# Attention and a three-layer chain on one core: TensorE in program order in one stretch

## The chip, the cores and the metric

The kernel runs on one core of a Trainium2 chip. The metric is the device time of one execution in microseconds, as the median of several runs. The engines have a queue each and work side by side: TensorE (PE in the rows; PEld are its weight loads) multiplies matrices and transposes, VectorE (DVE), ScalarE (ACT) and GpSimd (POOL) work on rows, SyncE (SP) issues most DMAs. Semaphores hold an instruction back until its inputs are there or its output buffer is free.

## The reference

Three layers follow each other.

```python
# 1 attention, B=4 batches, 8 heads, 512 local and 32 global tokens, 64 wide
out_g = softmax(q_g @ [k_g; k_l].T / 8) @ [v_g; v_l]
out_l = softmax([q_l @ k_g.T, masked(q_l @ k_l.T)] / 8) @ [v_g; v_l]   # |i-j| <= 32
x = concat(out_g, out_l)                  # 4 * 544 rows of 512
# 2 two products
x = leaky(x @ w_in) @ w_out               # 512 -> 2048 -> 512, leaky(h) = max(0.01 h, h)
# 3 soft mixture, 8 experts with 4 slots each
logits = x @ phi                          # 32 columns
d = softmax over rows (logits)            # dispatch, needs all rows
slots = d.T @ x
y = relu(slots @ w1[e]) @ w2[e]           # per expert
return softmax over columns (logits) @ y
```

## The kernel before

**Work and tiles.** The 2176 rows are 17 tiles of 128: tiles 0 to 15 are four per batch, tile 16 holds the global tokens of all batches. Layer 2's second product is never made for itself. With U = d.T @ leaky(h) and a matrix pmat = w_out @ phi that is made beforehand, the logits come from leaky(h) directly (`lg`), and U is summed over the tiles with a running maximum.

**Attention** goes by steps of a batch and a pair of heads (`step`, 4 per batch). `a_T` transposes k and q (tiles kTp and qTp), `a_S` makes 32 small products (sc, L434), each with 32 queries and a window of 96 keys and 32 global ones. VectorE masks them and takes the maximum (L446), ScalarE makes eight exponentials (L454). `a_E` transposes those (etp, copied out as eT), `a_V` makes 32 small products with v (po, L493). In the third step of a batch `g_S` makes the logits of global attention (gl, gg); after the fourth `g_E` transposes its exponentials (get, geg: L561, L565) and `g_V` multiplies (gpo, L579) and transposes the result (gxt, L592).

**A tile of layers 2 and 3.** `b_X` transposes a tile of x (xtp) and splits it in a coarse and a fine part. `b_H` makes H for a quarter f of 512 columns: 12 products of 128x512 in a bank hp (L691), in two half pieces of six, then ScalarE's Prelu (L698). For two quarters of a tile `blocks` transposes on VectorE and copies on GpSimd; `b_L` transposes the other two on TensorE (gtp). `b_D1` sums the logits (lg, L742) and copies them as lp. `b_D2` multiplies lp once more (L757), takes the running maximum (L761 on VectorE) and makes the exponential st (L766 on ScalarE, part of it copied by L767 on VectorE). `b_D3` transposes st (L802) and cuts out d; `b_U` multiplies d with the tile's g (up, L812) and adds it to U.

**Order.** `b_items` writes a list of items of weight and function for tiles 4 to 14: the half pieces h[0] to h[7] of a tile's H, and between them li[0] to li[5], the logits and U of the tile before: li[1] is `b_L`, li[2] to li[5] are `b_D1`, `b_D2`, `b_D3` and `b_U`; li[0] does nothing for these tiles. `merge` interleaves the steps of attention for batches 2 and 3 with that list by their weights. That is only the order of the program text. A scheduler then sets the order of every engine's queue by its own estimate of times, and puts what is ready in front of what waits; `held` and `behind` keep an item behind a named TensorE instruction. The last branch of `b_items` is for tiles 5 to 10, those beside attention.

**Buffers** on which the order bears: the transposes xtp, kTp, qTp, etp, gtp, get, geg and gg share two PSUM banks (`tp`), H and a few up share two (`hb`), sc and gl two (`sc`), po, gpo and the later up one (`po`).

Of the kernel before, what the change touches and what calls it, by code (L numbers as in the profile page):

```python
# [20 lines left out]
def kernel(  # L21
# [16 lines left out]
    B, H, S, D = q_l.shape  # L38
# [4 lines left out]
    NT = S // P  # L43
# [220 lines left out]
    class Stream:  # L264
# [15 lines left out]
        def next(self, dst=None, half=None):  # L280
            self.start()
            self.ahead = max(self.ahead - 1, RING)
            r = convert(self.pool, self.raw.pop(0), dst, half)
            return r
# [343 lines left out]
    def step(n):  # L628

        b, i = order[n]  # L630
        last = i == NP - 1
        e = (0.9, lambda: a_E(b, i))
        v = (1.6, lambda: (a_V(b, i), None if n < NP else load_vn(b) if i == NP - 2 else load_v(n + (1 if last else 2))))
        ns = [(2.7, lambda: a_S(*order[n + 1]))] if n + 1 < NN else []
        nt = [(0.9, lambda: T_(n + 2))] if n + 2 < NN else []
        if not last:
            gs = [(2.2, lambda: g_S(b))] if i == NP - 2 else []
            return ns + [e] + gs + nt + [v]
        gv = (2.1, lambda: (g_V(b), load_v(n + 2) if b else None))
        return [e, (0, lambda: None), v, (1.1, lambda: g_E(b))] + ns + nt + [gv]  # L640
# [11 lines left out]
    def b_X(t):  # L652
        if seq[t] is None:
            pt = xg0.rearrange("p k t -> p (k t)")
        else:
            b, T = seq[t]
            pt = tp("xtp")
            for i in range(KD):
                nc.tensor.transpose(  # L659
                    pt[:, P * i:P * i + P],  # L660
                    xn[b][:, T, 2 * i:2 * i + 2, :].rearrange("p h d -> p (h d)"), ident,
                )
        pool, tags = (sa, ("qn", "kn")) if t == 2 else (sb, ("xh", "xl"))
        xh, xl = (pool.tile([P, KD, P], F32R, tag=g, name="x" + g, bufs=2) for g in tags)
        nc.scalar.mul(xh.rearrange("p k t -> p (k t)"), pt, WS)  # L665
        nc.vector.scalar_tensor_tensor(
            out=xl.rearrange("p k t -> p (k t)"), in0=pt, scalar=WS,
            in1=xh.rearrange("p k t -> p (k t)"), op0=ALU.mult, op1=ALU.subtract,
        )
        xt[t] = (xh, xl)  # L670
# [3 lines left out]
    def b_H(t, f, half=None):  # L674
        xh, xl = xt[t]
        if half != 1:
            if f == 0:
                gt[t] = (
                    xa.tile([P, FF], F32, tag="xn", name="gx", bufs=1) if t in (3, NTT - 1)
                    else sa.tile([P, FF], F32, tag="vw", name="g2", bufs=2) if t == 2  # L680
                    else sb.tile([P, FF], F32, tag="g", name="g", bufs=2)
                )
            hps[0] = hb("hp")
        hp = hps[0]
        w = wi[f]
        lo, hi = {None: (0, KD), 0: (0, KD // 2), 1: (KD // 2, KD)}[half]
        prods = [(k, a, c) for k in range(lo, hi) for a, c in ((xh, 0), (xh, 1), (xl, 0))]
        if t == NTT - 1:
            prods.sort(key=lambda x: -x[2])
        for n, (k, a, c) in enumerate(prods):  # L690
            nc.tensor.matmul(  # L691
                hp, a[:, k, :], w[c][:, k, :],
                start=(n == 0 and half != 1), stop=(n == len(prods) - 1 and half != 0),
            )
        if half == 0:
            return
        gs = gt[t][:, 512 * f:512 * f + 512]
        nc.scalar.activation(out=gs, in_=hp, func=AF.Prelu, alpha=0.01)  # L698
        if t in BLK or t in HALF and f < 2:
            blocks(t, f, gs)  # L700
# [196 lines left out]
    def l_items(t):  # L897
        return ([(0.0, lambda: None), (0.6, lambda: b_M(t, range(2)))] if t in BLK else [
            (0.0, lambda: None) if t in HALF else (0.9, lambda: (b_L(t, 0), b_L(t, 1))),
            (0.9, lambda: (b_L(t, 2), b_L(t, 3))),  # L900
        ]) + [
            (1.3, lambda: b_D1(t)),
            (0.3, lambda: b_D2(t)),
            (0.1, lambda: b_D3(t)),
            (1.0, lambda: b_U(t)),
        ]
# [49 lines left out]
    def behind(item):  # L956
        def go():
            with tc.issue_after(ms["b"]):
                item[1]()
        return (item[0], go) + item[2:]  # L960

    def held(item):
        def go():
            with tc.issue_after(last_a[0]):
                item[1]()
        return (item[0], go)

    def b_items(t0, t1):
        its = []
        for t in range(t0, t1):  # L970
            li = l_items(t - 1)
            h = [held((1.3, lambda t=t, f=f, a=a: b_H(t, f, a))) for f in range(NQ) for a in range(2)]
            x = [(0.5, lambda t=t: b_X(t + 1), t + 1)] if t + 1 < NTT else []
            if t == NT:
                its += h[0:4] + x + h[4:]
                continue
            if t - 1 in BLK:
                its += h[0:2] + [li[1]] + h[2:4] + [li[2]] + x + [behind(h[4])]
                its += [li[3]] + [behind(x) for x in h[5:8]] + [li[4], li[5]]
                continue  # L980
            its += h[0:2] + [li[0]] + h[2:4] + [li[1]] + h[4:5] + x + h[5:6]
            its += [li[2], h[6], li[3], h[7], li[4], (0.0, lambda: None), li[5]]
        return its

    def merge(a, c):
        ta, tb = sum(x[0] for x in a) or 1.0, sum(x[0] for x in c) or 1.0
        pa = pb = 0.0
        a, c = list(a), list(c)
        while a or c:
            if a and (not c or pa / ta <= pb / tb):  # L990
                w, f = a.pop(0)[:2]
                pa += w
            else:
                w, f = c.pop(0)[:2]
                pb += w
            f()
# [20 lines left out]
    def run(*items):  # L1017
        for x in items:
            x[1]()
# [48 lines left out]
    attn = [None] + [sum((step(n) for n in range(NP * b, NP * b + NP)), []) for b in range(2, B)]  # L1068
    LB = NTT - 2
    rest = b_items(NT, LB)  # L1070

    def upto(t):
        n = next(n for n, x in enumerate(rest) if x[2:] == (t,))
        head = rest[:n]
        del rest[:n]
        return head

    for b in range(2, B):
        head = upto(b * NT if b == 2 else 3 * NT - 1)
        merge(attn[b - 1], head[:-6])  # L1080
        run(*head[-6:])
    actx.close()


# [93 lines left out]
    li = l_items(LB - 1)  # L1178
# [140 lines left out]
    for m, (c0, c1) in enumerate(((0, CL), (CL, 512))):  # L1319
# [24 lines left out]
        for n, ts in enumerate(order2):  # L1344
# [17 lines left out]
            else:  # L1362
                ob = obp.pop(0).rearrange("p (t c) -> p t c", c=W)
                copy(ob, opv)
                b, T = seq[ts[0]]
# [39 lines left out]
```

## Time and profile before

| | |
|---|---|
| median of 3 runs | 492.21 us (492.15 to 493.1) |
| profiled execution | 493.25 us, its span 491.5 us |
| TensorE busy in the span | 457.3 us (93%) |
| VectorE, ScalarE, GpSimd busy | 272.2, 232.8, 159.5 us |
[...]

The loop over batches 2 and 3 is the stretch from 189.0 to 344.4 us after the start of the span. [...] The difference of two starts in the timeline is the time that a group really took; a length beside a start reaches a little into the next group, because products are pipelined.

### The profile page before, as it was taken

How to read it: one execution, taken by the hardware profiler on the slowest of the kernel's cores; microseconds unless marked ns; L12 is line 12 of the kernel's file. 1: busy time of each engine (PE TensorE's matmuls, PEld its weight loads, DVE VectorE, ACT ScalarE, POOL GpSimd, SP SyncE). 2: the span in 40 equal slices, each digit the busy share in tenths (PEclk: the TensorE clock that was granted, in tenths of full speed). 3: DMA queues.
4: the chain of work that ended last, by engine and by line, in shares of the span. 5: the costliest groups of instructions: out<-in, count | busy, mean ns of one | idle time of the engine just before them, and what ended most of it. 6: DMA issues, size and time to landing. Idle time of an engine off the chain costs nothing.

```text
span 491.5 us, 13458 instructions
## 1 busy us (share of the span) xinstructions
PE 457.3 (93%) x5341; PEld 319.0 (65%) x5341; DVE 272.2 (55%) x880; ACT 232.8 (47%) x678; POOL 159.5 (32%) x281
## 2 busy tenths in 40 slices
PE   7967789998989999999999999999999999999982
PEld 5645568676766666776777776877777777743341
DVE  4676868489547676566554646435755542242223
ACT  4766889487754444445155526224533343321021
POOL 2044877333310202632415251515766630000000
PEclk9987889999989999999999999999999999999998
DMA  9989597499654565442450211229720059989997
GB/s 178 228 200 264 191 290 299 155 308 298 209 145 104 117 145 91 101 103 79 110 108 2 59 40 22 87 91 394 289 86 1 2 184 342 391 324 398 349 305 255
DMA packets 111990, 90.23 MB, mean 184 GB/s; under 512 B 75256, under 2 KB 94392, under 8 KB 111928
## 3 DMA queue, kind: packets, MB, share of 16 engines
q1 hardware_dynamic: 110024, 88.33, 61.5%
q10 hardware_dynamic: 1904, 1.05, 0.8%
q8 instruction: 42, 0.69, 0.6%
q14 instruction: 20, 0.16, 0.1%
HBM read 76.68 MB, written 8.65 MB: 174 GB/s over the span
## 4 chain that ended last, share of the span: by engine, by line
PE 77%; DVE 4%; ACT 3%; DMA 3%; issue 1%; SPq 1%; POOL 0%; DVEq 0%; ACTq 0%; POOLq 0%
PE hp L691 39%; PE gtp L728 4%; PE sc L434 3%; PE up L812 3%; PE ehp L1269 3%; PE po L493 3%; PE lg L742 3%; PE etp L473 2%; PE sop L1303 1%; PE gpo L579 1%; DMA wo_f<-wo 1%; PE qTp L390 1%; PE sop L1325 1%; PE lg L916 1%; PE xtp L659 1%; PE gl L519 1%
## 5 line engine op out<-in xcount | busy, mean ns | idle before, releaser
L691 PE MATMUL hp<-wi,xxh 128*128 128x512 f32 x512 | 167.2, 407 | 1.3 <-ACT xxh L665 1.3
L691 PEld LDWEIGHTS hp<-wi,xxh 128*128 128x128 f32 x512 | 91.8, 190 | 28.9 <-issue 9.1
L719 POOL COPY g<-gb 32x256 f32<-32x256 f32 x206 | 82.9, 402 | 82.6 <-DVE gb L710 55.5
L691 PE MATMUL hp<-wi,xxl 128*128 128x512 f32 x256 | 101.2, 396 | 0.0
L698 ACT ACTIVATE g<-hp 128x512 f32<-128x512 f32 x60 | 35.4, 597 | 57.9 <-PE hp L691 56.0
L454 ACT ACTIVATE se<-se,nmx 128x128 f32<-128x128 f32 x128 | 49.6, 391 | 21.2 <-DVE nmx L452 21.1
L691 PEld LDWEIGHTS hp<-wi,xxl 128*128 128x128 f32 x256 | 48.3, 189 | 11.9 <-issue 0.8
L200 POOL COPY vw<-vw 32x1664 f32<-32x1664 f32 x10 | 15.8, 1576 | 79.5 <-DMA vw<-in_v_l_dram 24.6
L446 DVE CUSTOM_DVE_ANT_0 se<-sc,mask 128x128 f32<-128x128 f32 x128 | 28.9, 284 | 12.1 <-PE sc L434 12.0
L261 POOL TENSOR_TENSOR wn<-wn,rraw 128x512 int32<-128x512 int32 x16 | 22.6, 1424 | 34.4 <-DVE wn L257 31.1
L710 DVE STREAM_TRANSPOSE gb<-g 128x512 f32<-128x512 f32 x32 | 22.3, 704 | 19.3 <-ACT g L698 14.0
L434 PE MATMUL sc<-kw,qT 64*32 64x128 f32 x1024 | 29.1, 283 | 0.4 <-DVE mx L446 0.4
L493 PE MATMUL po<-vw,eT 128*32 128x64 f32 x1024 | 23.7, 228 | 3.9 <-issue 3.2
L261 POOL TENSOR_TENSOR wo<-wo,rraw 128x512 int32<-128x512 int32 x12 | 15.7, 1310 | 32.3 <-DVE wo L257 8.9
L434 PEld LDWEIGHTS sc<-kw,qT 64*32 64x32 f32 x1024 | 19.8, 109 | 8.4 <-issue 5.4
L493 PEld LDWEIGHTS po<-vw,eT 128*32 128x32 f32 x1024 | 17.8, 113 | 10.4 <-issue 8.8
L477 DVE COPY eT<-etp 128x512 f32<-128x512 f32 x28 | 18.7, 685 | 10.0 <-PE etp L473 9.9
L454 ACT ACTIVATION_READ_ACCUMULATOR se<-se,nmx 128x1 f32 x128 | 24.2, 189 | 0.0
L473 PE MATMUL etp<-identr,se 128*128 128x128 f32 x128 | 22.7, 297 | 0.3
L405 DVE COPY kw<-kT 128x672 f32<-128x672 f32 x32 | 19.5, 644 | 3.1 <-ACT kT L394 2.9
L251 ACT ACTIVATE rraw<-rraw 128x512 int32<-128x512 uint32 x28 | 18.7, 681 | 4.0 <-POOL wo L261 2.8
L730 ACT COPY gT<-gtp 128x512 f32<-128x512 f32 x26 | 14.8, 586 | 10.8 <-PE gtp L728 7.0
(228 smaller groups left out, 764.7 us busy)
## 6 DMA issues: line engine op xcount, KB each, us to landing
ew<-in_moe_w_dram SPq DMA_DIRECT2D x23, 1024.0 KB, 8.4
rraw<-in_moe_w_in_dram SPq DMA_DIRECT2D x16, 512.0 KB, 6.4
ew<-in_moe_w_dram SPq DMA_DIRECT2D x15, 512.0 KB, 8.8
vw<-in_v_l_dram SPq DMA_DIRECT2D x60, 112.0 KB, 3.5
rraw<-in_moe_w_out_dram SPq DMA_DIRECT2D x12, 512.0 KB, 5.8
wo_f<-wo SPq DMA_DIRECT2D x16, 256.0 KB, 3.7
vn<-in_v_l_dram SPq DMA_DIRECT2D x4, 1024.0 KB, 6.2
wo<-wo_f SPq DMA_DIRECT2D x4, 1024.0 KB, 7.8
```

The source lines that it names most:

```text
L261: nc.gpsimd.tensor_tensor(out=di, in0=di, in1=m, op=ALU.add)
L405: nc.vector.tensor_copy(kw[:, :, 0:96], src)
L434: last_a[0] = nc.tensor.matmul(bks[e][32 * u:32 * u + 32, P * T:P * T + P], qt[64 * e:64 * e + 64, 32 * U:32 * U + 32], kw[win(U) // (NW / ...
L446: nc.vector.tensor_tensor_reduce(out=s[:, T, :], in0=bk[:, P * T:P * T + P], in1=mask[:, 0 if T == 0 else 2 if T == NT - 1 else 1, :], sca ...
L454: exp_last[0] = nc.scalar.activation(out=s[:, T, :], in_=s[:, T, :], func=AF.Exp, bias=nmx[:, e, T:T + 1], accum_out=sm[:, T, e:e + 1],).ins
L473: last_a[0] = nc.tensor.transpose(pt[:, P * T:P * T + P], es[e][:, T, :], ident).ins
L493: last_a[0] = nc.tensor.matmul(pov[32 * u:32 * u + 32, T, e, :], ets[e][:, 32 * U:32 * U + 32], vw[:, win(U), e, :], start=True, stop=True ...
L691: nc.tensor.matmul(hp, a[:, k, :], w[c][:, k, :], start=(n == 0 and half != 1), stop=(n == len(prods) - 1 and half != 0),)
L698: nc.scalar.activation(out=gs, in_=hp, func=AF.Prelu, alpha=0.01)
L710: nc.vector.transpose(out=gb[:, f % 2], in_=gs)
L719: copy(dst[32 * c:32 * c + 32, :, a], src[32 * a:32 * a + 32, :, c])
L728: nc.tensor.transpose(pt[:, P * c:P * c + P], g[:, o:o + P], ident)
```

## The change

Two edits. The items of tiles 5 to 10 are put in another order, and the loop over batches 2 and 3 is traced inside a block in which the scheduler leaves TensorE's queue in program order. The other engines' queues are still set by the scheduler.

```diff
@@ b_items, tiles 5 to 10
-            its += h[0:2] + [li[0]] + h[2:4] + [li[1]] + h[4:5] + x + h[5:6]
-            its += [li[2], h[6], li[3], h[7], li[4], (0.0, lambda: None), li[5]]
+            its += [h[0], li[1], h[1], li[0], h[2], h[3], li[2]] + x + [h[4], li[3]]
+            its += [h[5], h[6], li[4], h[7], li[5]]
@@ the loop over batches 2 and 3
-    for b in range(2, B):
-        head = upto(b * NT if b == 2 else 3 * NT - 1)
-        merge(attn[b - 1], head[:-6])
-        run(*head[-6:])
+    with tc.manual_schedule(engines={mybir.EngineType.PE}):
+        for b in range(2, B):
+            head = upto(b * NT if b == 2 else 3 * NT - 1)
+            merge(attn[b - 1], head[:-6])
+            run(*head[-6:])
```

First place: TensorE's queue where global attention of batch 2 ends. Before, the transposes of global attention's exponentials (get, geg) stand apart, the second pair behind passes of sc and lg:

```order
L434 MATMUL sc_3648<-kw,qT 32x128
L434 MATMUL sc_3647<-kw,qT 32x128
L434 MATMUL sc_3648<-kw,qT 32x128
L742 MATMUL lg<-g_3101,pmat 32x128 x8
L561 MATMUL get<-identr,gs 128x128 x4
L565 MATMUL geg<-identr,gs 32x128
L742 MATMUL lg<-gT,pmat 32x128 x8
L691 MATMUL hp<-wi,xxh 128x512 x2
```

In the changed program the same transposes, and those of the next tile of x, read:

```order
L561 MATMUL get<-identr,gs 128x128 x4
L565 MATMUL geg<-identr,gs 32x128
L561 MATMUL get<-identr,gs 128x128 x4
L565 MATMUL geg<-identr,gs 32x128
L659 MATMUL xtp<-identr,xn 128x128 x4
L691 MATMUL hp<-wi,xxh 128x512 x2
```

The sc and lg that lay between have moved: sc stands undivided behind the half piece of H that follows, lg undivided ahead.

Second place: a little later on TensorE, where st of tile 6 is transposed (L802) and global attention's result too (gxt). Before:

```order
L434 MATMUL sc_3919<-kw,qT 32x128
L434 MATMUL sc_3920<-kw,qT 32x128
L434 MATMUL sc_3919<-kw,qT 32x128
L592 MATMUL gxt<-identr,xg 128x128
L802 MATMUL lg<-identr,st 128x128
L728 MATMUL gtp<-identr,g 128x128 x4
L434 MATMUL sc_3920<-kw,qT 32x128
```

After, from the last products of the sc of the step before (3661 and 3662) up to L802:

```order
L434 MATMUL sc_3661<-kw,qT 32x128
L434 MATMUL sc_3662<-kw,qT 32x128
L757 MATMUL lg<-lp,s_77 128x128
L691 MATMUL hp<-wi,xxh 128x512 x2
L691 MATMUL hp<-wi,xxl 128x512
L691 MATMUL hp<-wi,xxh 128x512 x2
L691 MATMUL hp<-wi,xxl 128x512
...
L390 MATMUL kTp<-identr,kn 128x128 x4
L390 MATMUL qTp<-identr,qn 128x128 x4
L802 MATMUL lg<-identr,st 128x128
```

Four more rows of H (the second half piece) stand where the line of dots is. Behind L802 come a half piece of H, the whole of gpo and then gxt:

```order
L691 MATMUL hp<-wi,xxl 128x512
L579 MATMUL gpo<-vn,get 32x64 x16
L579 MATMUL gpo<-vg,geg 32x64 x4
L579 MATMUL gpo<-vn,get 32x64 x16
L579 MATMUL gpo<-vg,geg 32x64 x4
L592 MATMUL gxt<-identr,xg 128x128
L812 MATMUL up<-g,d 32x512 x4
```

What moved: the passes of the next sc lie no longer between gpo and gxt or around L802, and L802 stands two half pieces of H and two transposes behind L757, where before gpo, qTp, a half piece and passes of sc lay between them.

Third place: ScalarE's queue at the same point. The eight exponentials of attention (se) are those of the sc above. Before:

```order
L454 ACTIVATE se,sm<-se,nmx 128x128 x8
L665 ACTIVATE xxh<-xtp 128x512
L394 ACTIVATE kT<-kTp 128x512
L766 ACTIVATE st,zt<-lg,nm 128x128
L771 ACTIVATE al<-al 128x1
```

After:

```order
L454 ACTIVATE se,sm<-se,nmx 128x128 x8
L766 ACTIVATE st,zt<-lg,nm 128x128
L771 ACTIVATE al<-al 128x1
L394 ACTIVATE kT<-kTp 128x512
L394 ACTIVATE qT<-qTp 128x512
```

st has moved up to the place right behind the eight; kT is behind it now.

## Rows read from the trace of the kernel before

**Rows 1.** The page's chain of waits, shares of the span by engine.

```profile
PE 77%; DVE 4%; ACT 3%; DMA 3%; issue 1%; SPq 1%; POOL 0%; DVEq 0%; ACTq 0%; POOLq 0%
```

**Rows 2.** Windows: length; busy PE, PEld, DVE, ACT, POOL; clock, DMA share, GB/s.

```profile
160.00:189.00 29.00, 27.38 (x540) 16.82 (x539) 20.50 (x72) 12.37 (x45) 4.72 (x3) 1.00 0.67 137
189.00:344.40 155.40, 155.01 (x1963) 113.86 (x1965) 84.67 (x318) 65.24 (x223) 58.34 (x125) 1.00 0.37 98
344.40:400.00 55.60, 55.60 (x374) 41.13 (x367) 34.04 (x90) 23.37 (x61) 35.53 (x88) 1.00 0.24 88
142.34:145.74 3.40, 3.40 (x23) 2.36 (x25) 0.89 (x2) 0.76 (x2) 0.00 (x0) 0.50 0.88 217
```

**Rows 3.** Timeline of TensorE: start, us, operation; visits to narrow shapes.

```profile
195.64 0.32 PE L493 MATMUL po<-vw,eT 128*32 128x64 f32 x8
195.89 0.66 PE L390 MATMUL qTp<-identr,qn 128*128 128x128 f32 x4
...
202.92 1.16 PE L434 MATMUL sc<-kw,qT 64*32 64x128 f32 x64
204.01 0.72 PE L691 MATMUL hp<-wi,xxh 128*128 128x512 f32 x2
...
233.88 0.41 PE L434 MATMUL sc<-kw,qT 64*32 64x128 f32 x4
234.22 0.73 PE L691 MATMUL hp<-wi,xxh 128*128 128x512 f32 x2
...
237.17 0.44 PE L434 MATMUL sc<-kw,qT 64*32 64x128 f32 x14
237.54 1.10 PE L493 MATMUL po<-vw,eT 128*32 128x64 f32 x64
238.57 1.09 PE L728 MATMUL gtp<-identr,g 128*128 128x128 f32 x8
...
266.68 0.70 PE L742 MATMUL lg<-gT,pmat 128*32 128x128 f32 x13
267.31 0.73 PE L691 MATMUL hp<-wi,xxh 128*128 128x512 f32 x2
```

**Rows 4.** Groups by line, 189 to 345 us: busy us, mean ns, idle before.

```profile
L757 PE MATMUL lg<-lp,s 128*128 128x128 f32 x12 | 2.5, 292 | 0.0
...
L563 DVE COPY get<-get 128x512 f32<-128x512 f32 x4 | 2.7, 687 | 6.6 <-PE get L561 6.6
...
L587 DVE TENSOR_TENSOR xg<-gpo,grs 128x128 f32<-128x128 f32 x2 | 0.6, 284 | 2.2 <-PE gpo L579 2.2
```

**Rows 5.** Timeline of TensorE: a half piece of H, then eight transposes.

```profile
205.49 0.62 PE L691 MATMUL hp<-wi,xxh 128*128 128x512 f32 x2
...
206.88 1.04 PE L473 MATMUL etp<-identr,se 128*128 128x128 f32 x8
207.67 0.71 PE L691 MATMUL hp<-wi,xxh 128*128 128x512 f32 x2
```

**Rows 6.** Timeline of TensorE and ScalarE: exponentials of attention, and st.

```profile
191.69 0.39 PE L691 MATMUL hp<-wi,xxl 128*128 128x512 f32 x1
...
192.00 0.40 ACT L454 ACTIVATE se<-se,nmx 128x128 f32<-128x128 f32 x1 [3.83 <-DVE nmx L452]
...
195.10 1.06 ACT L698 ACTIVATE g<-hp 128x512 f32<-128x512 f32 x2
...
206.19 0.39 ACT L454 ACTIVATE se<-se,nmx 128x128 f32<-128x128 f32 x1
...
226.12 0.37 ACT L766 ACTIVATE st<-lg,nm 128x128 f32<-128x128 f32 x1 [3.12 <-DVE gmx L531]
...
227.14 0.33 PE L802 MATMUL lg<-identr,st 128*128 128x128 f32 x1
```

**Rows 7.** Timeline of TensorE: two idle stretches, in brackets.

```profile
142.08 0.91 PE L728 MATMUL gtp<-identr,g 128*128 128x128 f32 x4 [1.29 <-DVE gT L730]
...
179.77 0.66 PE L561 MATMUL get<-identr,gs 128*128 128x128 f32 x4 [0.98 <-DVE get L563]
```

## The prediction

> **What bounds the kernel now.** I read the chain of waits first. TensorE holds 77% of it and DMA 3% [rows 1], so what counts is how TensorE's instructions follow each other. The changed loop runs from 189.0 us, where the first pieces of tile 4's H start, to 344.4. By the busy time in that stretch TensorE works 155.0 of 155.4 us at full granted clock, while VectorE works 84.7 and ScalarE 65.2 [rows 2]. So no wait worth removing is left there: at most the 0.4 us of idleness. The next 55.6 us are filled to the last digit [rows 2], so whatever the loop gains or loses is handed on one for one. In the tail the loads are let go by TensorE's own progress, and DMA's small share of the chain gives no slack that could take a shift up.
>
> A busy TensorE can still be slow. The timeline shows what one interruption costs. Each visit to the narrow shapes (sc, po, lg, up, gl, gpo) is paid on the way in and out. Undivided, the 64 passes of a po take 1.03 us (237.54 to 238.57) and those of an sc 1.09 (202.92 to 204.01), 0.016 and 0.017 a pass. Cut up, 8 passes of po take 0.25, 4 of sc 0.34, 14 of sc 0.37 and 13 of lg 0.63 [rows 3]. Less their passes, the visits cost 0.12, 0.27, 0.13 and 0.41 us.
>
> **The change part by part.** The amount of work is the same: both programs hold the same instructions in the loop, and only their order differs. The scheduler that interleaved them is kept off TensorE's queue, so sc, po, gl and gpo now stand whole, and the new list of items puts lg, its two small steps and up between half pieces of H.
>
> *Saved.* In the order of TensorE's instructions over this loop I count 51 entries into a narrow shape before and 26 now. The mean of the four visits is 0.23 us, so 25 fewer save 5.8 us; by the cheapest 3.0, by the dearest 10.3. I take the mean, since the cut pieces are of all these sizes. With the 0.4 us of idleness, 6.2.
>
> *New waits.* TensorE's queue has no filler any more, so each chain over another engine must fit into what stands between its two ends.
>
> (a) The transpose of st (L802). In batch 2's last step a whole sc comes first, then L757, two half pieces, kTp and qTp, then L802. That is 0.3 us for L757's pass pair [rows 4], 1.39 for each half piece and 0.79 for eight transposes [rows 5]: 3.9 us. On the other side, ScalarE starts the eight exponentials 2.18 us after the sc (204.01 to 206.19), they take 3.10 (192.00 to 195.10), and from st's own exponential to the transpose it took 1.02 (226.12 to 227.14) [rows 6]. The st exponential stands behind the eight in ScalarE's queue, so this is a sum: 6.3. Wait: 2.4 us. One tile later the same chain has xtp, three half pieces, L757 and eight transposes to hide behind, about 5.7, and a copy of etp also stands ahead of st's copy on VectorE: 0.7. Behind the waiting transpose are the second half piece of H, gpo and up, so nothing covers it. Together 3.1; if the exponentials were not in the way 0, and at most 4.
>
> The eight exponentials do hold up what stands behind them: the first H piece ended at 191.69 + 0.39, and its Prelu began at 195.10, when the eight were through [rows 6]. [...] Were it otherwise, st would be ready 3.2 us after the sc, TensorE would not wait there, the clock term below would go too, and the sum would be 1.0 us of gain.
>
> (b) Global attention's transposes: get, geg, get, geg and xtp now follow each other on two banks, and each get leaves its bank by a copy of 0.69 us on VectorE [rows 4]. The nearest row is the wait of this very kind before the loop, 0.98 [rows 7]. Less work stands on VectorE's queue here, so I take 0.75 for the second get and 0.65 for xtp; in batch 3 an L802 stands in xtp's place and only 0.75 remains. 2.15, between 1 and 3.
>
> (c) gxt right behind gpo, twice: xg's multiplication takes 0.28 [rows 4] and is handed over twice. Before, passes of sc lay in between. 0.5 each, 1.0, between 0.6 and 1.6.
>
> (d) etp, etp, gtp, gtp in a row, twice: the third needs the first one's bank, whose copy (0.69) is longer than the four transposes beside it (0.4). 0.5 each, 1.0, between 0 and 2.
>
> (e) xtp behind kTp and qTp twice, where ScalarE works a bank off in about half a microsecond (two in 1.06 from 195.10) [rows 6], xtp behind two etp once, and up once behind eight mask instructions on VectorE: 1.0 for all, between 0 and 2.
>
> Sum of the waits 8.25.
>
> *The clock.* [...] Half of 3.4 us is lost, less the little that is a wait anyway: 1.6. Without a fall 0, with two 3.2.
>
> *Sum.* 8.25 + 1.6 - 6.2 = 3.65, say 3.7 us slower. The profiled execution took 493.25 us, 491.5 of span and 1.75 around it, so it would become 496.9. It lies 1.04 above the median of the runs; from 492.21 I come to 495.9. Attention's last step ends earlier than now (fewer visits ahead of it, H pieces behind), so the four loads of wo that wait for gxt are issued earlier; nothing needs them before the tail, and they bring nothing.
>
> **Rivals.**
> *The clock stays up.* [...] Then 8.25 - 6.2 = 2.1 us slower: 494.3.
> *A second fall.* The waits of (b) lie two within some 2 us and make 1.4 together; if the clock falls there as well, 5.3 us slower, and with waits 0.7 dearer 498.2.
> *Faster: the changes of shape are the real cost.* The place is every boundary between H or transposes and a narrow tile. At the dearest visit in the rows, 0.41, 25 visits are worth 10.3 and with the idleness 10.7, against waits of 8.25 without a fall: 2.4 us faster, 489.8. It decides from 0.31 a visit without a fall, from 0.38 with one. For it speaks lg's visit, against it those of po and of sc's 14 passes. [...]
> *No change.* A visit at about 0.31 and no fall balance: 492.2. Also, if the waits on st were much shorter than their parts add up to.
>
> **How the numbers follow.** The forecast with one fall has a chance of 0.40, its own range being 494.4 to 497.4 (visits from 0.17 to 0.29). No fall 0.20, a second fall or dearer waits 0.12, no change 0.12, faster 0.16. A measurement of this kernel can tell about 0.2%, 1 us, from no change. Part of "no fall" lies within it: slower 0.69, same 0.14, faster 0.17. The range of eight in ten leaves out the far half of the faster case and the far end of a second fall: 490.5 to 499.3.
>
> **What would show it.** In the profile after, TensorE's waits should name st's copy (L767) in front of L802 with 2 us or more at one place and under 1 at another, get in front of get, xg in front of gxt; the granted clock should show 0.50 for about 3.4 us some 60 us into the loop. Whole groups of 64 passes for po and sc should be seen, and the loop's busy time should shrink by some 6 us while its idle time grows from 0.4 to about 8. I am wrong if L802 finds st ready, if a visit costs another price than 0.23, or if the end of attention in batch 2 is not the place where TensorE stands longest.

## The result, and the profile after

The changed kernel took 496.19 us in the median of four runs (495.39 to 497.15), the kernel before 492.2 beside it: a ratio of 1.0077, 95% interval 1.0056 to 1.0099. In a second series the two stood at 497.81 and 492.36, a ratio of 1.0111 (1.0081 to 1.0142). The change makes the kernel about 0.9% slower. The profiled execution took 497.15 us, 495.4 of it span; before it was 493.25 and 491.5. The mean granted clock of the two executions is 0.968 and 0.975.

Below, "the loop" is the stretch from the first half piece of H behind 186 us to the first logits product of the tile that follows attention, some 360 products of H later. Before, it ran from 189.07 to 344.34 us (155.3), after from 188.25 to 347.86 (159.6). So the loop became 4.3 us longer. The part ahead of it was 0.8 shorter in this execution and the part behind it 0.4 longer, which gives the 3.9 us of the two spans.

Chain of waits, the page of the changed kernel:

```profile
PE 65%; DVE 8%; ACT 4%; DMA 3%; SPq 1%; issue 1%; POOL 1%; DVEq 0%; ACTq 0%; POOLq 0%
```

TensorE held 77% of it [rows 1]; the points that it lost went to VectorE and ScalarE above all, since the chain now runs through the waits for them. Windows of the changed kernel (columns as in [rows 2]), the loop, the stretch of half speed in it, and what follows:

```profile
188.25:347.86 159.61, 150.06 (x1963) 114.62 (x1964) 88.86 (x319) 65.30 (x223) 58.08 (x125) 0.99 0.39 108
252.15:255.56 3.41, 3.06 (x11) 2.02 (x15) 2.10 (x8) 0.94 (x2) 0.00 (x0) 0.50 0.13 29
347.86:403.00 55.14, 55.14 (x371) 40.75 (x364) 33.94 (x89) 23.36 (x61) 35.35 (x88) 1.00 0.14 51
```

TensorE is busy 150.1 of 159.6 us, against 155.0 of 155.4 [rows 2]: idle time has grown from 0.4 to 9.5 us, and busy time has gone. From the end of the loop to 403 us it is busy to the last digit, so nothing was given back there. What it waited for in the loop (in total, times, longest):

```profile
PE lg L802 <- DVE st L767: 3.8, 2, 3.1
PE get L561 <- DVE get L563: 1.4, 2, 0.7
PE gxt L592 <- DVE xg L587: 0.9, 2, 0.5
PE up L812 <- ACT gs L536: 0.8, 1, 0.8
PE gtp L728 <- DVE eT L477: 0.7, 2, 0.3
PE xtp L659 <- DVE get L563: 0.7, 1, 0.7
PE xtp L659 <- ACT kT L394: 0.6, 2, 0.3
PE xtp L659 <- DVE eT L477: 0.3, 1, 0.3
PE up L812 <- DVE d L789: 0.3, 1, 0.3
```

The narrow groups stand whole, where [rows 3] has them cut up. TensorE's timeline of the changed kernel, a po, 12 products of H and an sc (the kernel's text makes 32 products of po and of sc, and the profile counts 64; a pass is one of these):

```profile
198.05 1.10 PE L493 MATMUL po<-vw,eT 128*32 128x64 f32 x64
...
202.02 1.16 PE L434 MATMUL sc<-kw,qT 64*32 64x128 f32 x64
```

And the longest wait, on TensorE, VectorE, GpSimd and ScalarE. The scores of step 12 end at 245.32:

```profile
244.23 1.16 PE L434 MATMUL sc<-kw,qT 64*32 64x128 f32 x64
...
252.50 0.48 PE L802 MATMUL lg<-identr,st 128*128 128x128 f32 x1 [3.06 <-DVE st L767]
252.63 1.20 PE L691 MATMUL hp<-wi,xxh 128*128 128x512 f32 x2
253.63 0.63 PE L691 MATMUL hp<-wi,xxl 128*128 128x512 f32 x1
```

```profile
247.12 0.29 DVE L761 TENSOR_REDUCE nm<-lg 128x1 f32<-128x128 f32 x1
247.33 1.15 DVE L452 TENSOR_SCALAR nmx<-mx 128x4 f32<-128x4 f32 x2
...
252.16 0.28 DVE L767 COPY st<-lg 32x128 f32<-32x128 f32 x1
```

```profile
246.81 1.57 POOL L200 COPY vw<-vw 32x1664 f32<-32x1664 f32 x1
```

```profile
248.51 0.40 ACT L454 ACTIVATE se<-se,nmx 128x128 f32<-128x128 f32 x1 [0.67 <-DVE nmx L452]
...
251.60 0.34 ACT L766 ACTIVATE st<-lg,nm 128x128 f32<-128x128 f32 x1
```

ScalarE works off the eight exponentials of step 12 from 248.51 to 251.60 and only then takes st's. TensorE stands from 249.44 to 252.50. The two H rows behind the wait take 1.00 us for two products and 0.43 for the third, where at a granted clock of 1.00 such rows took 0.54 and 0.23 in the same trace (242.67 to 243.21, and to 243.44): the clock stands at 0.50 from 252.15 to 255.56, as the window shows.

### The profile page after: what moved, and what is told of

Same layout as the page of the kernel before. It is cut to its first block, busy times and chain, and to the rows that moved or that the text cites. A ratio compares the mean times of both kernels' runs of the same rounds, so it can differ in the third digit from the quotient of the medians.

```text
span 495.4 us, 13462 instructions
## 1 busy us (share of the span) xinstructions
PE 452.7 (91%) x5341; PEld 319.9 (65%) x5341; DVE 277.2 (56%) x880; ACT 232.9 (47%) x678; POOL 160.3 (32%) x281
## 4 chain that ended last, share of the span: by engine, by line
PE 65%; DVE 8%; ACT 4%; DMA 3%; SPq 1%; issue 1%; POOL 1%; DVEq 0%; ACTq 0%; POOLq 0%
PE hp L691 31%; PE gtp L728 4%; PE sc L434 3%; PE up L812 3%; PE po L493 2%; PE lg L742 2%; PE ehp L1270 2%; DMA ew<-in_moe_w_dram 2%; DVE se L446 2%; PE etp L473 2%; ACT se L454 2%; PE sop L1304 1%; SPq L1127 1%; PE wotp L345 1%; PE gpo L579 1%
## 5 line engine op out<-in xcount | busy, mean ns | idle before, releaser
L691 PEld LDWEIGHTS hp<-wi,xxh 128*128 128x128 f32 x512 | 93.3, 193 | 28.3 <-issue 6.6
L454 ACT ACTIVATE se<-se,nmx 128x128 f32<-128x128 f32 x128 | 49.6, 390 | 15.6 <-DVE nmx L452 15.5
L434 PE MATMUL sc<-kw,qT 64*32 64x128 f32 x1024 | 27.5, 283 | 1.2 <-DVE kw L406 0.5
L493 PE MATMUL po<-vw,eT 128*32 128x64 f32 x1024 | 21.9, 229 | 2.8 <-issue 2.0
```

The source lines that it names most:

```text
L434: last_a[0] = nc.tensor.matmul(bks[e][32 * u:32 * u + 32, P * T:P * T + P], qt[64 * e:64 * e + 64, 32 * U:32 * U + 32], kw[win(U) // (NW / ...
L454: exp_last[0] = nc.scalar.activation(out=s[:, T, :], in_=s[:, T, :], func=AF.Exp, bias=nmx[:, e, T:T + 1], accum_out=sm[:, T, e:e + 1],).ins
L493: last_a[0] = nc.tensor.matmul(pov[32 * u:32 * u + 32, T, e, :], ets[e][:, 32 * U:32 * U + 32], vw[:, win(U), e, :], start=True, stop=True ...
L691: nc.tensor.matmul(hp, a[:, k, :], w[c][:, k, :], start=(n == 0 and half != 1), stop=(n == len(prods) - 1 and half != 0),)
```

## The experiments

All figures of the loop are from the profiled execution of each kernel, worked out from its timeline as said above: its length, TensorE's idle time, the entries into a narrow shape (visits; the transposes geg are not counted as one), and the time at half speed in it. Ratios are to runs of the kernel before on the same chip.

| kernel | median us | ratio (95%) | loop us | idle | visits | half speed |
|---|---|---|---|---|---|---|
| before | 492.2 to 493.2 | 1 | 155.3 | 0.4 | 51 | 0 |
| changed | 496.19 | 1.0077 (1.0056 to 1.0099) | 159.6 | 9.5 | 26 | 3.4 |
| changed, again (c_after) | 497.81 | 1.0111 (1.0081 to 1.0142) | 159.9 | 9.6 | 26 | 3.4 |
| new list, scheduler (e1_list) | 495.98 | 1.0056 (1.0031 to 1.0081) | 158.0 | 2.2 | 47 | 0 |
| old list, program order (e2_program_order) | 509.93 | 1.0306 (1.0259 to 1.0354) | 167.5 | 15.5 | 28 | 6.8 |
| st first (e3_st) | 493.14 | 1.0001 (0.9977 to 1.0025) | 156.0 | 7.4 | 26 | 0 |
| wait filled (e4_fill) | 496.08 | 1.0059 (1.0037 to 1.008) | 158.5 | 6.9 | 26 | 0 |
| waits covered (e5_waits) | 483.69 | 0.982 (0.9791 to 0.9849) | 147.4 | 0.7 | 25 | 0 |
| the same, again (c_e5) | 484.78 | 0.9838 (0.9799 to 0.9877) | 146.9 | 0.4 | 25 | 0 |
| joined (e6_joined) | 484.72 | 0.9824 (0.9795 to 0.9853) | 146.6 | 1.3 | 17 | 0 |
| po cut in two (e7_visits) | 500.19 | 1.0143 (1.0106 to 1.0181) | 163.3 | 9.7 | 33 | 6.8 |
| covered list, scheduler (e8_sched) | 495.84 | 1.0051 (1.0025 to 1.0078) | 158.8 | 1.9 | 49 | 0 |
| both (e9_both) | 483.74 | 0.9808 (0.9769 to 0.9847) | 145.6 | 0.8 | 17 | 0 |

Single runs of one kernel lie up to 7 us apart, those of the kernel before from 490.0 to 496.8, and the profiled executions differ by up to 4 us in when the loop begins. So a difference of 1 or 2 us is read from the loop in the trace rather than from the medians.

**Each edit alone.**

```diff
 e1_list: the new list, the loop without the block
-    with tc.manual_schedule(engines={mybir.EngineType.PE}):
-        for b in range(2, B):
+    for b in range(2, B):
 e2_program_order: the block, with the old list in b_items
```

> The new list of a tile's items, but TensorE's order in the loop left to the scheduler as before. My account of the change (a cost of 9.5 us of waits of TensorE in program order and 1.4 us of clock, a gain of some 6 us of fewer visits to narrow shapes) makes the cause the fixed order: with the scheduler the waits are filled again and the visits are cut up again, so the time is that of before, 491.5 to 493. Rival: it is the new list that puts the logits and U of a tile too early for their data, whoever orders TensorE; then this run stays near the changed kernel, 494.5 to 496.5.

> TensorE in program order, but with the old list, in which a tile's st transposes stand one half piece behind the product that st is made from (two in the new list), and U straight behind them. My account: U then waits for d in each of six tiles, some 0.6 us each, and the st transposes wait oftener, so waits of 12 to 15 us in place of 9.5 and a time of 498 to 501: the new list is what makes the fixed order bearable. Rival: the list makes no difference, 495.5 to 497.

The first run fits neither theory. Its time, 495.98, lies where the rival put it, but the rival's reason is not there: with the scheduler the waits are filled, to 2.2 us, and the visits are cut up again, to 47; yet the loop takes 158.0 us and not 155.3. The scheduler makes a worse order of the new list than of the old one. TensorE's timeline of that kernel shows one part of it: the products gl of batch 3 are torn into two halves (by the kernel's text one head each, rows 0 to 63 or 64 to 127 of kT), with L802 between them.

```profile
300.34 1.06 PE L519 MATMUL gl<-kT,qgT 64*32 64x512 f32 x8
301.34 0.33 PE L802 MATMUL lg<-identr,st 128*128 128x128 f32 x1
301.60 1.06 PE L519 MATMUL gl<-kT,qgT 64*32 64x512 f32 x8
```

Before, all 16 passes stood together and took 1.09, so this costs 1 us:

```profile
299.59 1.09 PE L519 MATMUL gl<-kT,qgT 64*32 64x512 f32 x16
```

With 1.8 us more idle time that is 2.8, of which four visits fewer should give back some 1.3 (an estimate, at 0.32 each as worked out below). About 1.2 of the 2.7 us stays unexplained.

The second run shows that the fixed order is the dear edit and the new list what makes it bearable: 15.5 us of idle time, and 2.8 us for half speed (152.0 us busy with 28 visits, against 148.6 with 26 in e3_st, which had none). Its waits and its window of half speed:

```profile
PE lg L802 <- DVE st L767: 6.5, 2, 4.5
PE etp L473 <- ACT gT L730: 2.5, 1, 2.5
PE gxt L592 <- DVE xg L587: 1.8, 2, 1.4
```

```profile
301.39:308.22 6.83, 5.54 (x18) 2.90 (x19) 2.48 (x10) 1.02 (x7) 0.00 (x0) 0.50 0.00 0
```

My 498 to 501 had U's wait (1.7 us, where 3.6 were expected) as the main thing; it was st again, with waits up to 4.5 us, and the clock. The profiled run was near the lowest of its six (504.6 to 511.1). The four slower ones show a mean granted clock of 0.949 to 0.958, the two fastest 0.963 and 0.966, so more half speed than the trace shows goes with the median of 509.93; where it lay is open.

**The wait on st, and the clock.**

```diff
 e3_st: in the order of batch 2's items
-    ... x of tile 7, h[4], scores of step 12, b_D2 of tile 5, h[5], h[6] ...
+    ... x of tile 7, h[4], b_D2 of tile 5, scores of step 12, h[5], h[6] ...
 e4_fill: in b_D3, for tile 5, ahead of the transposes
+            w = hb("w")
+            for n in range(12):
+                nc.tensor.matmul(
+                    w, xt[t + 1][0][:, n % KD, :], wi[3][0][:, n % KD, :],
+                    start=True, stop=True, skip_group_check=True,
+                )
```

> The changed kernel with one item moved: the product that st of tile 5 is made from stands ahead of the scores of attention step 12 in place of behind them, so that st's exp stands ahead of the eight attention exps in ScalarE's queue. My account: the wait of 3.06 us at the st transposes goes, and with it the fall of the clock (1.4 us), so 496.2 - 4.5 = 491.7 (491.2 to 492.4). Rival 1: the clock falls elsewhere all the same, 493.1. Rival 2: the wait only moves, since the eight exps and what needs them come later, 495 to 496.5.

> The changed kernel with twelve products of 128x512 more, of operands that H uses and into a bank that nobody reads, ahead of the st transposes of tile 5: TensorE works through the wait of 3.06 us, which stays as long. My account (the clock falls because TensorE stands idle there): the granted clock stays at 1.0 in the loop and the half piece behind the wait takes 1.5 us in place of 2.84, so 496.2 - 1.4 = 494.8 (494.4 to 495.3). Rival: the clock's fall has another cause (the load of the stretch, the time since the last fall), and the time stays at 495.9 to 496.7 with the clock at 0.5 for some 3.4 us.

With st first the wait is gone, and the granted clock is 1.00 over the loop (186.83 to 342.87). TensorE's timeline of e3_st, with L757 ahead of the sc:

```profile
242.80 0.38 PE L757 MATMUL lg<-lp,s 128*128 128x128 f32 x2
243.12 1.16 PE L434 MATMUL sc<-kw,qT 64*32 64x128 f32 x64
...
247.93 0.27 PE L802 MATMUL lg<-identr,st 128*128 128x128 f32 x1
```

The loop is 3.6 us shorter, not 4.5: the wait at gxt grew from 0.51 to 1.39. ScalarE and VectorE show why:

```profile
250.24 0.57 ACT L394 ACTIVATE kT<-kTp 128x512 f32<-128x512 f32 x1
```

```profile
250.84 1.02 DVE L405 COPY kw<-kT 128x672 f32<-128x672 f32 x2
...
252.22 0.28 DVE L587 TENSOR_TENSOR xg<-gpo,grs 128x128 f32<-128x128 f32 x1
```

The eight exponentials, which begin at 247.14, now end after L802, kT's copy stands right behind them, and VectorE copies the next step's windows (kw) from it ahead of xg, which begins only at 252.22; gpo had ended near 251.25. In the changed kernel those copies were through at 254.61, before gpo ended. That is rival 2 in a small part. The ratio, 1.0001 against 1.0077 and 1.0111 for the changed kernel, is 3.7 to 5.4 us less. The median, 493.14, lies where rival 1 stood (493.1), but its fall of the clock is not in the trace.

With the wait filled, TensorE works through it and nothing else changes:

```profile
248.69 3.01 PE L805 MATMUL w<-wi,xxh 128*128 128x512 f32 x12
252.04 0.33 PE L809 MATMUL lg<-identr,st 128*128 128x128 f32 x1 [0.34 <-DVE st L767]
252.12 0.71 PE L691 MATMUL hp<-wi,xxh 128*128 128x512 f32 x2
252.67 0.39 PE L691 MATMUL hp<-wi,xxl 128*128 128x512 f32 x1
```

The granted clock is 1.00 from 189 to 347 us, the two products of H behind the wait take 0.55 (252.12 to 252.67) where the changed kernel's took 1.00, and the loop is 158.5 us, 1.1 and 1.3 shorter than in the two traces of the changed kernel; 1.4 was expected. The median (496.08) doesn't show it: it lies in the rival's range, and the interval of its ratio overlaps with that of the changed kernel's first series. The traces show the fall where TensorE stands idle there (0.50 for 3.41 us in the changed kernel and in c_after) and none where it is busy; the gain in time is not shown by the medians.

> The changed kernel again, so that the kernels of this series are compared with it on one chip. Expected as before: 495.5 to 497, a ratio of 1.006 to 1.010 to the kernel before; in its trace the waits of TensorE in the loop are 9.5 us again, since they follow from the order and from durations. What is open is the clock: if its fall at the st transposes belongs to the wait of 3.06 us, it is there again.

The control repeated the waits to a few hundredths (3.06, 0.51, 0.77, 0.68) and the half speed behind st's (here at 256.26, behind a wait that ended at 255.36).

**All waits covered.** No work changes; get and geg, and gpo and gxt, are items of their own now. S, T, E, V are scores, transposes, weights and values of an attention step; h, L1, D1 to D3, U those of the tile list, with the tile whose H they stand beside; X.t makes the x of tile t+1; L0 is the item that does nothing; gS, gE, gV, gX global attention's (gE0 and gE1 its two heads):

```diff
-T.10 X.4 h4.4 V.8                               (batch 2)
+T.10 h4.4 X.4 V.8
-h7.4 h0.5 E.9 L1.5 h1.5
+h7.4 E.9 h0.5 L1.5 h1.5
-gS.2 D3.5 h7.5 U.5
+D3.5 gS.2 h7.5 U.5
-V.11 h3.6 D1.6 gE.2 X.6 h4.6 S.12 D2.6 h5.6
+V.11 gE0.2 h3.6 D1.6 X.6 h4.6 D2.6 S.12 gE1.2 h5.6
-gV.2 gX.2 U.6
+gV.2 U.6 gX.2
-D3.7 h7.7 T.14 U.7 V.12                         (batch 3)
+h7.7 D3.7 T.14 V.12 U.7
-T.15 X.8 h4.8
+T.15 h4.8 X.8
-S.15 D3.8 h7.8 U.8 h0.9 E.14 L1.9 gS.3 h1.9
+D3.8 S.15 h7.8 U.8 E.14 h0.9 L1.9 h1.9 gS.3
-E.15 X.9 h4.9 V.15 D2.9 h5.9 h6.9 gE.3 D3.9 h7.9 gV.3 gX.3 U.9
+E.15 h4.9 X.9 V.15 D2.9 gE0.3 h5.9 gE1.3 h6.9 gV.3 D3.9 h7.9 gX.3 U.9
```

> The changed kernel with each item that waits set where other work covers it: the product for st of tile 5 ahead of the scores of step 12, the st transposes of tile 6 a half piece later, those of tiles 4 and 7 ahead of the global and the local scores that they stood behind, the two halves of the transposes of the global weights (get, geg) apart, gxt behind U or a half piece behind gpo, xtp and gtp a half piece away from the four transposes before them. No work is added or taken out. My account: the waits fall from 9.5 to under 1 us, the clock stays up (1.4), and one visit less (U straight behind gpo, 0.25): the loop takes 148.5 to 149.5 us in place of 159.6 (before 155.3), and the time is 486 to 488.5 where the kernel before has 492 to 493. Rival: the attention chain through VectorE and ScalarE is the real bound of the loop, so the waits come back at other places, 4 us or more of them, 490 to 493.

> The kernel with the waits covered once more, as the yardstick of this series: 482.5 to 485, a loop of 147.4 us with 0.7 us of idle time of TensorE and 25 visits.

The loop falls to 147.4 and 146.9 us. All the waits that are left, and the loop's window:

```profile
PE gxt L601 <- DVE cs L809: 0.5, 1, 0.5
PE qTp L390 <- ACT gs L542: 0.2, 1, 0.2
```

```profile
187.77:335.18 147.41, 146.73 (x1963) 113.53 (x1965) 86.41 (x320) 65.33 (x223) 58.12 (x125) 1.00 0.42 117
```

The rival is out: VectorE and ScalarE, busy 86.4 and 65.3 us, keep up with a TensorE that is idle for 0.7 of 147.4. The time, 483.7 and 484.8, is lower than I expected, and the windows show why. The busy time is 146.7, against 148.6 in e3_st, with one visit fewer. The idle column counts too little. In the changed kernel etp, gtp and H follow each other like this:

```profile
205.99 1.03 PE L473 MATMUL etp<-identr,se 128*128 128x128 f32 x8
207.37 1.32 PE L728 MATMUL gtp<-identr,g 128*128 128x128 f32 x8 [0.35 <-DVE eT L477]
208.44 0.47 PE L691 MATMUL hp<-wi,xxh 128*128 128x512 f32 x1
```

and with the waits covered like this:

```profile
203.89 1.04 PE L473 MATMUL etp<-identr,se 128*128 128x128 f32 x8
204.68 0.71 PE L704 MATMUL hp<-wi,xxh 128*128 128x512 f32 x2
...
206.16 1.03 PE L741 MATMUL gtp<-identr,g 128*128 128x128 f32 x8
206.95 0.71 PE L704 MATMUL hp<-wi,xxh 128*128 128x512 f32 x2
```

By the starts the two groups took 2.45 us there and 0.79 + 0.79 here. So the wait cost 0.87, and the bracket shows 0.35. The bracket counts from the end that the profile gives the instruction before, 205.99 + 1.03 = 207.02, and the profile's key calls the ends of matmuls modelled: with the waits covered H starts at 204.68, 0.25 ahead of the end that etp is given (203.89 + 1.04).

**The price of a visit.**

```diff
 e7_visits: a_V in two items, with a half piece of H between, for seven steps
+        v0 = (0.0, lambda: a_V(b, i, range(2)))
-        v = (1.6, lambda: (a_V(b, i), ...
+        v = (1.6, lambda: (a_V(b, i, range(2, NT)), ...
```

> The changed kernel with seven of its eight runs of weights-times-values products (po x64) cut in two, 32 and 32, with a half piece of H between: as many products, seven visits to a narrow shape more. My account: 7 x 0.25 = 1.75 us more busy time of TensorE in the loop, waits as in the changed kernel give or take 0.5, and a time 1.5 to 2.2 us over the changed kernel in the same series (497.5 to 499). Rival: the saved busy time came from something else that the scheduler's cutting did (transposes cut up, products of one row group left alone), and a cut of po alone costs under 0.05 us: within 0.5 us of the changed kernel.

TensorE's timeline of it:

```profile
196.63 0.65 PE L494 MATMUL po<-vw,eT 128*32 128x64 f32 x32
...
198.82 0.65 PE L494 MATMUL po<-vw,eT 128*32 128x64 f32 x32
...
200.99 0.34 PE L434 MATMUL sc<-kw,qT 64*32 64x128 f32 x8
```

Six products of H stand behind each half. From the first po to the sc it takes 4.36 us, where the whole po of the changed kernel and the same 12 products take 3.97 (198.05 to 202.02): 0.39 for the cut. For all seven: the loop is 3.5 us longer than the mean of the two of the changed kernel; some 0.9 of that is half speed that lasted 6.8 us instead of 3.4 (252.32 to 257.99 here, 255.45 to 260.18 in c_after, for the same products), and 0.15 idle time. That leaves 2.4, or 0.35 a cut. The rival's price of a cut, under 0.05, is out, and the price is higher than the 0.25 I had expected (the median, 500.19, lies above my 497.5 to 499). That the scheduler's cutting had other costs beside it is not out: the torn gl in e1_list is one.

**Narrow runs joined, and both.**

```diff
 e6_joined, on the order with the waits covered; four of the eight places
-V.8 h5.4 h6.4 S.10
+h5.4 V.8 S.10 h6.4
-V.9 h3.5 S.11 D1.5
+h3.5 V.9 S.11 D1.5
-D3.5 gS.2 h7.5 U.5 T.12 h0.6 V.10
+D3.5 gS.2 U.5 V.10 h7.5 T.12 h0.6
-S.15 h7.8 U.8
+S.15 U.8 h7.8
 e9_both, on that
-h0.5 L1.5 h1.5 T.11 L0.5 h2.5
+h0.5 h1.5 T.11 h2.5 L1.5 L0.5
-T.13 D3.6 h7.6 gV.2
+D3.6 h7.6 T.13 gV.2
-L1.8 h1.8 L0.8 h2.8 E.13
+E.13 h1.8 L1.8 h2.8 L0.8
```

> As the run with the waits covered, and the narrow shapes (sc, po, lg, up, gl) set beside each other, so that the loop has 17 visits to them in place of 25, each with as many products as before. My account (0.25 us a visit, from 154.9 - 148.6 us of busy time for 51 - 26 visits): 2.0 us less than that run, a loop of 146.5 to 148 us and a time of 484 to 487. Rival 1: the price is not paid by the visit, so the busy time stays at 148.4. Rival 2: attention steps that follow each other so closely wait for their windows and weights (VectorE), 2 us or more, and the time is 487 to 490.

> The joined kernel (17 visits) with the three places mended at which its trace still shows a wait (0.22, 0.29 and 0.66 us, each with some 0.2 us that the modelled ends hide): the transposes of tile 4's H behind attention step 11's, step 13's transposes a half piece later, step 13's weights ahead of tile 7's transposes. My account: the loop takes 145 to 146 us in place of 146.6, so 1.5 to 2.5 us less than the kernel with the waits covered in the same series, 481 to 483.5. Rival: the joined runs bring waits at other places, and the loop stays at 146.5 or more: within 0.8 us of it.

Joined, the busy time falls by 1.4 us against e5_waits for eight visits, 0.18 each, less than the 0.25 expected, and the idle time rises by 0.6: rival 2 in part. With the three waits mended the loop takes 145.6 us, the shortest of all, as expected; but its 483.74 can't be told from the 484.78 beside it. Both orders beat the kernel before by 1.6 to 1.9% and the changed one by more.

**Does the fixed order matter once the list is right?**

> The list with the waits covered, but TensorE's order in the loop left to the scheduler. My account: the scheduler cuts the narrow runs up again wherever it can (some 20 visits more, 0.3 us each) and gives back 6 us, 488 to 492. Rival: what counted was the list; with no wait to fill the scheduler leaves the runs whole, 483 to 486.

It does. Left to the scheduler, the covered list takes 158.8 us in the loop with 49 visits and 1.9 us of idle time, and 495.84 us in all, about as with the new list alone. That is 11.6 us over the mean of the two covered loops. As an estimate, its 24 visits more account for 7.7 at 0.32 each and the idle time for 1.4. Of the other 2.5, gl gives some 1.2: it is torn here too, and by the starts of the instructions, less the idle time shown, it takes 3.00 us in this loop and 1.76 in that of e5_waits. The rest is not explained. TensorE is busy 2.0 us longer here than in the kernel before, with two visits fewer, so the number of visits does not set the busy time alone. My estimate, 6 us given back, was too low.

## Why the prediction was right, step by step

The forecast of 495.9 us came within 0.3 of the first series, and the mechanism was the one predicted. So close a hit is luck in part: the second series was 5.4 us slower than the kernel before, where 3.7 were forecast, and two terms of the sum were both too small and partly cancel.

*Saved.* 25 visits at 0.23 came to 5.8 us. The price is not one number. From 51 visits before to 26 in e3_st, neither with half speed in the loop, the busy time fell from 154.9 to 148.6 us: 6.3, or 0.25 a visit. To 25 with the waits covered it fell to 146.6 (the mean of the two runs): 8.3, or 0.32 a visit, 8.0 for 25. Counted by the starts of the instructions, less the idle time shown, 5.5 of these 8.3 us went at the narrow shapes (with the two small steps of lg), 0.75 at H and 2.0 at the transposes; at the transposes there can be waits that the modelled ends hide, in the kernel before too. So 8.0 is the upper figure. That the narrow shapes are where it was saved is plain: po took 9.67 us before and 8.11 in the changed kernel, sc 7.82 and 6.52, lg 10.01 and 7.67. The cut of po gave 0.35, the joining 0.18. The prediction took a mean of four visits in [rows 3]; its bounds, 0.12 to 0.41, hold all of these. These figures give a visit as a whole; how the price divides between the way in and the way out no run shows. It named another price than 0.23 as a sign of being wrong: the size was off by that sign, but not the mechanism.

*Waits.* Predicted 8.25 us, shown 9.5. (a) st: 3.83 (3.06 and 0.77) for 3.1. The chain was right, but the exponentials began 3.2 us after the sc (245.32 to 248.51) and not 2.18 [rows 6]. VectorE set nm's reduction between the masks and nmx, which is 0.2 of it. The rest is nmx itself: its two instructions took 1.15 us, where in the kernel before they took

```profile
205.81 0.29 DVE L452 TENSOR_SCALAR nmx<-mx 128x4 f32<-128x4 f32 x2
```

The long one ran until 248.41, and GpSimd's copy of vw until 248.38, beside it. In e3_st, where that copy was nearly through when nmx began, nmx took 0.44. That the copy held it up is not shown by a run of its own. So the 3.1 for (a) was too small.

(b) get and xtp: 2.03 for 2.15. (c) gxt: 0.92 for 1.0. (d) gtp behind etp: 0.70 shown for 1.0. (e) xtp and one up: 1.22 for 1.0. Not predicted: 0.79 at up of tile 4 (225.70 to 226.49). The trace names ScalarE's gs, but up doesn't read it; it needs d, which VectorE copied from 226.16 to 226.34, behind the maxima of gl. Moving D3 ahead of gS took the wait away.

To the 9.5 may come what the modelled ends hide. From the changed kernel's loop to that with the waits covered it is 12.2 us; less 1.5 for the clock and 0.3 for a visit, 10.4 are left for waits, and 0.7 are still shown there: 11.1 us in all. This is worked out, not seen in one view, and it stands and falls with the 8.0 above: what isn't a visit there was a hidden wait before the change too.

*Clock.* 1.6 us predicted, one fall some 60 us into the loop for 3.4 us. It came at 252.15, 64 us into the loop, for 3.41 us, and cost 1.5 (busy time 150.06 against 148.60 in e3_st). The rival without a fall is out in both traces of the changed kernel, and so is a second fall in the loop. The 1.6 in the sum had one case to rest on: in the kernel before, 3.40 us at 0.50 began 0.26 us after the idle 1.29 us had ended at 142.08, while behind the idle 0.98 us that ended at 179.77 the clock stayed at 1.00 [rows 2, 7]. That the 2.4 us of (a), being longer than the 1.29, would bring a fall as well was my estimate. No run shows a fall behind a wait of that length: in e2_program_order waits of 2.00 and 2.49 us came without one, and the fall that cost 1.5 here came with a wait of 3.06. e4_fill, at 1.00 with the wait filled, ties it to the idle time; that it was called from 2.4 us is luck in part.

*Sum.* By what the traces show, 9.5 + 1.5 - 6.3 - 0.4 = 4.3; with the upper figures 11.1 + 1.5 - 8.0 - 0.4 = 4.2. The loop became 4.3 longer; predicted were 3.65. That either sum closes proves nothing, since its terms are differences of the same loops' lengths. The waits were too small by 1.3 us or more, the saving by 0.5 or more. The rival "faster" wanted 0.38 a visit with a fall; 0.25 to 0.32 is less, and even with 0.32 and the waits that were predicted the change would have cost 1.45 us (8.25 + 1.6 - 8.0 - 0.4).

*Why.* That st's exponential stands behind eight others in ScalarE's queue was the step with most at stake, and e3_st shows it: put ahead of them, it was ready without a wait (L802 at 247.93 has none). That transposes on two banks wait for copies is shown by the run with the waits covered, for all of them together and not one by one: behind get, eT and kT the changed kernel's transposes waited 3.7 us (1.4 + 0.7 + 0.7 + 0.6 + 0.3), and there 0.2 is left, at qTp. My wider reading ahead of e1_list, that a fixed order as such is what costs, was wrong: the same fixed order with another list makes the kernel 1.6 to 1.8% faster than before.

## What to carry to other kernels

A queue in fixed order that feeds three others is worth what its list is worth: read each wait that the trace names, put an item of independent work between its two ends, and check which instructions stand ahead of the producer in its own engine's queue. Judge the gain by the starts of instructions and the length of the stretch, not by the idle column. The order that suits a fixed queue is not the one that suits a scheduler, so the two edits are to be timed together and apart.

## What was not expected of the hardware

The idle stretch that [rows 7] show ahead of the loop stands at the same instruction in five other traces, and the clock fell at it in some only. In the kernel before, at 0.50 [rows 2], the next four transposes of gtp took 1.06 us, and in the changed kernel, at 1.00, 0.60. By that length it fell in c_after and c_e5 too (1.06 in both) and not in e3_st and e5_waits (0.60). The row in the changed kernel, in c_after, in e5_waits and in c_e5:

```profile
142.98 0.66 PE L728 MATMUL gtp<-identr,g 128*128 128x128 f32 x4 [1.35 <-DVE gT L730]
```

```profile
143.41 0.95 PE L728 MATMUL gtp<-identr,g 128*128 128x128 f32 x4 [1.46 <-DVE gT L730]
```

```profile
142.52 0.66 PE L741 MATMUL gtp<-identr,g 128*128 128x128 f32 x4 [1.43 <-DVE gT L743]
```

```profile
143.70 0.70 PE L741 MATMUL gtp<-identr,g 128*128 128x128 f32 x4 [1.38 <-DVE gT L743]
```

So in these traces the length of the idle stretch doesn't decide by itself: 1.34, 1.35 and 1.43 came without a fall, 1.29, 1.38 and 1.46 with one. The four longest waits in the loops of these kernels came with a fall: 3.06 in the changed kernel, 3.10 in e7_visits and 4.51 in e2_program_order during the wait, 3.06 in c_after 0.90 us after its end. The 1.39 at gxt in e3_st and the 2.00 and 2.49 in e2_program_order (L802 at 226.62, etp at 285.81) came with none, though both of the latter are longer than the 1.29 ahead of the loop that did [rows 7]. For the same wait the half speed lasted 3.41 us in two traces and 6.83 in e7_visits. This may be part of the spread of single runs of one kernel; no run here separates it.

Eight passes of gl, those of one head, take 1.06 us alone (e1_list), and sixteen, those of both heads, 1.09 together (the kernel before). The scheduler's order lost that gain where it set the two halves apart. A cut of po between products of H cost 0.35 us here; what this price is made of no run shows.
